# Attention feeding a gated mixture: reordering the first transfers, with batch 1 in half-size units

## The chip, the cores and the metric

The kernel runs on one core of one Trainium2 chip. The metric is the device time of one execution in microseconds (us). The profile is of one execution, with its engines: TensorE (PE, its weight loads PEld), VectorE (DVE), ScalarE (ACT), GpSimd (POOL) and SyncE (SP), which here only issues DMAs.

## The reference

Attention over 8 batches of 8 heads with 576 positions of 64 numbers, in a window of 128 with a linear bias, then a mixture of 8 experts over all 4608 tokens, whose gate is normalised over rows and columns in turn:

```
scores = scale * q @ k.T                      # per batch and head
scores = where(0 <= rel < 128, scores - slope[h] * |rel|, -1e9)
x = softmax(scores) @ v                       # (4608, 512) after joining the heads
P = exp(x @ w_gate - max)
8 times: P /= P.sum(1) + 1e-9;  P /= P.sum(0) + 1e-9;  P *= N / E
out = sum over e of P[:, e] * (relu(x @ w1[e]) @ w2[e])
```

## The kernel before, in words

Every engine's order is the order of the program: it is written out by hand, and the framework adds only waits and buffers. An engine that waits for one operand therefore holds up all that stands behind it.

**Attention.** A batch is 5 blocks of keys (four of 128 positions and a tail of 64), each in two halves of heads, so 10 steps. A step is named (b, at), with at = 0 to 9. Step n of the loop does, in order: the scores of the next steps (`scores`, L385, PE), their exponentials (`exps`, L403, ACT), about 1 us of expert work, the mask (`masks`, L416, DVE), the value products (`values`, L441, PE), the turn of the finished block into `xT` (`turn_x`, L472), and more expert work. Scores run one step or two ahead of the values. In `values`, the batch 0 steps and the first six of batch 1 begin with three spins: products of a constant tile (L225) whose result is written over, there to keep TensorE active. `spin_alone` adds more between the steps.

**q, k and v.** `load_qk` (L245, SP) brings q and k of a batch as two transfers of 1 MB. `cast_qk` (b, j) turns heads 2j and 2j+1 to 16 bits, k on ACT (L260) and q on DVE (L258); `turn_pe` turns them on PE (L324) with the copies on ACT (L339, k) and DVE (L337, q). v comes block by block (`load_v`, L347, SP; `cast_v`, L357 and L358, POOL), the tail of q and k by `load_tail` (L236, SP). In the main loop stand, of this kind: `load_v` six blocks ahead at odd steps, `load_qk(b + 2)` and its tail at (b, 3) and later from b = 1 on, the casts of batch 2 in batch 1, and **the first cast of batch 3 at the end of (1, 8)** (L722). Buffers of v and of the tails are five in number; a load waits until the one it takes is free.

**Experts 0 and 1** run beside the attention. Their weights W1 and W2 are loaded and cast by DMAs that POOL issues (L87, L89), each in POOL's order. A unit is one expert on a range of blocks (a block is 128 tokens): 8 layer-1 atoms of 128 hidden columns (L103: four products each, then a ReLU on ACT, L110), then one layer-2 atom per block (L116: eight products, then a copy on DVE). `Filler` hands atoms out: `take()` gives one layer-2 atom after two of layer 1, `fill(us)` goes on until that time is spent, `hold` keeps layer 2 back, `ready` says how many blocks of `xT` exist, `allowed` which experts. In batches 0 to 2 a step's share is the backlog divided by the steps left to at = 8. PSUM has four buffers for all of these products and the turns.

The units come in this order, where `spans` are ranges (first block, blocks):

```
spans = [(0, 2), (2, 2)] + [(4 * g, 4) for g in range(1, NG)]
order = [(0, 0), (0, 1)]
for n in range(2, len(spans)):
    order += [(0, n), (1, n - 2)]
```

**Ahead of batch 1's scores** the program runs the rest of expert 0 on batch 0, both layers, between the casts and turns of batch 1. The later part of the kernel (the gate, experts 2 to 7) isn't touched.

Of the kernel before, what the change touches and what calls it, by code (L numbers as in the profile page):

```python
# [14 lines left out]
def kernel(  # L15
# [10 lines left out]
    nc = tc.nc  # L26
# [4 lines left out]
    B, H, S, Dh = q.shape  # L31
# [10 lines left out]
    NKB = 5  # L42
# [162 lines left out]
    if True:  # L205
# [23 lines left out]
        def spin_alone(n):  # L229
            spins[0] += 1  # L230
            spin(aps.tile([P, GT], FP32, name=f"psJ_{spins[0]}", tag="pmm", bufs=4), n)
# [6 lines left out]
                )  # L238
            tails[b] = t32

        def load_qk(b):
            q32 = per.tile([P, H, RI * Dh], FP32, name=f"q32_{b}", tag="a8", bufs=8)
            k32 = per.tile([P, H, RI * Dh], FP32, name=f"k32_{b}", tag="a8", bufs=8)
            for t, src in ((q32, q), (k32, k)):
                nc.sync.dma_start(  # L245
                    out=t, in_=src[b, :, 0:SM, :].rearrange("h (p i) d -> p h (i d)", i=RI)
                )
            raw[b] = (q32, k32)

        def cast_qk(b, j):  # L250

            if j == 0:
                c16s[b] = per.tile([P, 2, RI, H, Dh], FP16, name=f"c16_{b}", tag="a8", bufs=8)
            for n in (1, 0):
                src = raw[b][n][:, 2 * j : 2 * j + 2, :].rearrange("p h (i d) -> p i h d", i=RI)
                to = c16s[b][:, n, :, 2 * j : 2 * j + 2, :]
                if n == 0:
                    nc.vector.tensor_copy(out=to, in_=src)  # L258
                else:
                    nc.scalar.copy(out=to, in_=src)  # L260
            if j == NDT - 1:
                raw.pop(b)

        def homes(b):
            qN = asb.tile([P, NDT, SM], FP16, name=f"qN_{b}", tag="qN", bufs=2)
# [156 lines left out]
        def values(b, kb, u):  # L422

            nk, _ = sizes(kb)
            if u == 0:
                xsbs[b, kb] = asb.tile([P, H, Dh], FP16, name=f"xsb_{b}_{kb}", tag="xsb", bufs=3)
            psN = aps.tile([P, GT], FP32, name=f"psN_{b}_{kb}_{u}", tag="pmm", bufs=4)
            if b == 0 or (b == 1 and 2 * kb + u < 6):
                spin(psN, 3)
            psN = psN[:, 0 : 4 * Dh + 4].rearrange("p (h d) -> p h d", h=4)  # L430
            ops = []
            for y in range(2):
                for hb in range(2):
                    hh = 2 * y + hb
                    if kb > 0:
                        ops.append((hh, pts[b, kb - 1, u][:, 2 * hb + y, P : P + nk], vs[b, kb - 1][:, 4 * u + hh, 0 : Dh + 1]))
                    ops.append((hh, pts[b, kb, u][0:nk, 2 * hb + y, 0:nk], vs[b, kb][0:nk, 4 * u + hh, 0 : Dh + 1]))
            if kb == NKB - 1:
                ops = ops[0::2] + ops[1::2]
            for i, (hh, lhsT, rhs) in enumerate(ops):  # L440
                nc.tensor.matmul(  # L441
                    out=psN[0:nk, hh, :],
                    lhsT=lhsT,
                    rhs=rhs,
                    start=(i == 0),
                    stop=(i == len(ops) - 1),
                )
            if kb > 0:
                pts.pop((b, kb - 1, u))
            rden = asb.tile([P, 4], FP32, name=f"rden_{b}_{kb}_{u}", tag="rden", bufs=2)  # L450
            nc.vector.reciprocal(out=rden[0:nk, :], in_=psN[0:nk, :, Dh])
            nc.vector.tensor_tensor(
                out=xsbs[b, kb][0:nk, 4 * u : 4 * u + 4, :],
                in0=psN[0:nk, :, 0:Dh],
                in1=rden[0:nk, :].unsqueeze(2).to_broadcast([nk, 4, Dh]),
                op=ALU.mult,
            )
# [59 lines left out]
            nc.vector.tensor_copy(out=yo, in_=ps)  # L517
            stores.append((e, blk, yo))

        spans = [(0, 2), (2, 2)] + [(4 * g, 4) for g in range(1, NG)]  # L520
        order = [(0, 0), (0, 1)]
        for n in range(2, len(spans)):
            order += [(0, n), (1, n - 2)]
# [91 lines left out]
        load_first()  # L615
        spin_alone(20)
        make_mask(range(4))
        cast_v(0)
        load_weights(0, 0, 1)
        cast_v(1)  # L620
        load_weights(0, 1, 2)
        cast_v(2)
        nc.gpsimd.dma_start(out=wg_sb, in_=moe_w_gate.rearrange("(dt p) e -> p dt e", p=P))
        cast_v(3)
        cast_v(4)
        load_qk(1)
        load_tail(1)
        load_v(NKB)


        steps = [(b, kb, u) for b in range(B) for kb in range(NKB) for u in range(2)]
# [18 lines left out]
        for n, (b, kb, u) in enumerate(steps):  # L650
            nxt = steps[n + 1] if n + 1 < len(steps) else None
            at = 2 * kb + u
            left = ((8 if b < XPE else 10) - at) % 10 + 1
            budget = filler.backlog() / (11 if (b, at) == (XPE, 0) else left)
            if b == 0:
                budget = 1.0 if at in (6, 7) else 0.0
            if nxt:
                if nxt[0] < XPE and nxt[1:] == (RI - 2, 1):
                    turn_pe(nxt[0], 0, NDT)
                if nxt == (1, 0, 0):  # L660
                    filler.ready = RI
                    while filler.l1 or filler.todo[0][1] < RI:
                        filler.take()
                    filler.hold = False
                    spin_alone(8)
                    filler.fill(3.6)
                    cast_qk(1, 0)
                    cast_qk(1, 1)
                    for j in range(NDT):
                        turn_pe(1, 1, j)  # L670
                        turn_pe(1, 0, j)
                        if j < 2:
                            cast_qk(1, j + 2)
                        filler.fill(1.0)
                if n == 0:
                    scores(*nxt)
                elif nxt[2] == 0:
                    scores(*nxt)
                    scores(*nxt[:2], 1)
                exps(*nxt)  # L680
            got = filler.fill(1.0) if b else 0.0
            if nxt:
                masks(*nxt)
            values(b, kb, u)
            if n > 0 and u == 0 and by_pe(steps[n - 1][0]):
                turn_x(*steps[n - 1][:2])
            if u == 1 and n // 2 + NKB < B * NKB:
                cast_v(n // 2 + NKB)
            filler.fill(budget - got)
            if at == 0 and b > XPE:  # L690
                filler.ready = 4 * b
            if at < 8 and b < XPE:
                filler.ready = 4 * b + at // 2
            if at == 8 and b < XPE:
                filler.ready = 4 * b + 4
            if u == 1 and not by_pe(b):
                turn_x(b, kb)
            if u == 1:
                if kb == 1 and b > 0:
                    gates(4 * b - 4, 4 * b)  # L700
                if n // 2 + NKB + 1 < B * NKB:
                    load_v(n // 2 + NKB + 1)
            if b == 0 and at == 1:
                load_weights(1)
            if b == 1 and at == 4:
                filler.allowed.add(1)
                nc.sync.dma_start(out=ysp[0, 0:RI].rearrange("m p d -> p m d"), in_=first_y[0])
            if (b, at) == (0, 3):
                load_qk(2)
            if (b, at) == (0, 7):  # L710
                homes(1)
            if (b, at) == (1, 3):
                homes(2)
            if b == 1 and 4 <= at <= 7:
                cast_qk(2, at - 4)
            if b == 1 and 5 <= at <= 8:
                turn_pe(2, 1, at - 5)
                turn_pe(2, 0, at - 5)
            if 1 <= b < B - 2 and at == 3:
                load_qk(b + 2)  # L720
            if 1 <= b < B - 2 and at >= 8:
                cast_qk(b + 2, at - 8)  # L722
            if 2 <= b < B - 1:
                if at < 2:
                    cast_qk(b + 1, at + 2)
                if at == 1:
                    turn_qk(b + 1)
                    order_qk(b + 1, 1, range(NDT))
                if at == 5:
                    turn_tail(b + 1)  # L730
                if at in (6, 7):
                    order_qk(b + 1, 0, range(2 * at - 12, 2 * at - 10))
            if b < B - 1 and at == (1 if b > 1 else 5) and b:
                load_tail(b + 1)
            if 10 * b + at >= 66:
                i = 10 * b + at - 66
                if i % 8 == 0:
                    home_last(2 + i // 8)
                (load_w2 if i % 8 < 4 else load_w1)(2 + i // 8, i % 4, 4)
            if (b, at) == (7, 0):  # L740
                todo += sums_of(2, *extras(2))
            if b == 7 and at >= 5:
                some(1)
# [334 lines left out]
```

## Time and profile before

| what | value |
|---|---|
| median of 3 runs | 1058.27 us (1057.51 to 1058.65) |
| the profiled execution's own time | 1056.82 us |
| its span | 1055.0 us |
| PE busy | 1037.6 us, 98% |
| ACT busy | 437.3 us, 41% |
| DVE busy | 631.4 us, 60% |
| POOL busy | 77.4 us, 7% |
| moved by DMA | 98.57 MB |
| k and q of batch 1 landed | 35.5 and 31.5 us |
| W1 and W2 of expert 0 landed | 22.4 and 30.3 us |
| W1 and W2 of expert 1 landed | 52.0 and 59.4 us |

A span is the time between the first and the last recorded instruction; the execution's own time has 1.8 us around it. "Idle before, releaser" in a row is the time that an engine stood before those instructions, and what ended it. "Issue to landing" of a DMA is the time from the start of the instruction that issues it until its last data are there. Starts are in us from the span's start. A matmul row's duration includes the pipeline, so a group of eight is shorter than eight times one; the chain's rows show what a group really takes.

### The profile page before, as it was taken

Reading aid. Unit: us, or ns where it says so; the run is one execution under the profiler, and the core shown is the slowest. Engines: PE = TensorE matmul, PEld = TensorE weight load, DVE = VectorE, ACT = ScalarE, POOL = GpSimd, SP = SyncE. Lnnn points to the kernel's source line nnn. Section 1 sums busy time; section 2 is a strip of 40 time slices with the busy share of each in tenths; the row PEclk is TensorE's granted clock in tenths of the full one; section 3 lists DMA queues with packets and bytes.
Section 4 is the critical chain, followed back from the end, with each engine's and each line's share of the span. In section 5 each row is a group of like instructions: output and inputs, shape, how many; then the busy total and the mean of one; then the engine's idle time right before and its main releaser. Section 6 shows DMA issues by size and latency. Waiting matters only on the chain.

```text
span 1055.0 us, 21321 instructions
## 1 busy us (share of the span) xinstructions
PE 1037.6 (98%) x9094; PEld 808.2 (77%) x9094; DVE 631.4 (60%) x1166; ACT 437.3 (41%) x734; POOL 77.4 (7%) x139
## 2 busy tenths in 40 slices
PE   8999999999999999999999999999999999999998
PEld 5664444454444888888888888888888888888887
DVE  5555666565687665655655655655655555556555
ACT  7655564655332333333333333333333333333332
POOL 2122033234100000000000000000000000000000
PEclk9999999999999999999999999999999999999999
DMA  9997488979991510210210220210220220220240
GB/s 227 248 226 170 105 216 201 202 152 188 180 204 56 106 47 25 71 52 21 71 61 11 71 64 8 71 53 19 71 69 3 71 70 2 71 71 1 71 90 21
DMA packets 166111, 98.57 MB, mean 93 GB/s; under 512 B 84960, under 2 KB 157440, under 8 KB 166016
## 3 DMA queue, kind: packets, MB, share of 16 engines
q1 hardware_dynamic: 151280, 79.21, 28.9%
q0 software_dynamic: 14304, 17.84, 10.2%
q8 instruction: 71, 1.16, 0.4%
q14 instruction: 24, 0.20, 0.1%
q10 hardware_dynamic: 432, 0.16, 0.1%
HBM read 87.74 MB, written 19.02 MB: 101 GB/s over the span
## 4 chain that ended last, share of the span: by engine, by line
PE 90%; DMA 6%; SPq 2%; DVE 1%; ACT 1%; issue 0%; POOL 0%; POOLq 0%; DVEq 0%; ACTq 0%
PE psh L865 35%; PE psS_m L920 31%; PE psy L116 10%; PE psh L103 10%; DMA v<-in_v_dram 4%; PE psN L441 1%; DMA xT<-xsb 1%; PE psS L385 1%; DMA pbc<-ptd 1%; SPq L347 1%; SPq L236 1%; ACT pt L403 0%; DVE yo L517 0%; PE psy L985 0%; DMA k<-in_k_dram 0%
## 5 line engine op out<-in xcount | busy, mean ns | idle before, releaser
L872 ACT ACTIVATE hs<-psh 128x512 f16<-128x512 f32 x432 | 257.9, 597 | 454.5 <-PE psh L865 372.9
L865 PE MATMUL psh<-aux,w1l 128*128 128x256 f16 x2880 | 372.6, 273 | 1.5 <-DVE aux L849 1.5
L865 PEld LDWEIGHTS <-w1l 128*128 128x128 f16 x2880 | 281.7, 98 | 34.5 <-issue 1.7
L920 PEld LDWEIGHTS <-hs 128*128 128x128 f16 x2568 | 251.3, 98 | 29.1
L877 DVE TENSOR_TENSOR hs<-hs 128x1024 f16<-128x1024 f16 x107 | 74.1, 693 | 274.4 <-ACT hs L872 274.4
L920 PE MATMUL psS_m<-w2l,hs 128*128 128x256 f16 x1440 | 186.6, 273 | 0.0
L103 PE MATMUL psh<-xT,w1t 128*128 128x512 f16 (+1 forms) x640 | 139.9, 358 | 2.2 <-ACT hT L110 1.4
L849 DVE TENSOR_TENSOR aux<-xT,pbc 128x1024 f16<-128x1024 f16 x108 | 131.4, 1218 | 3.8 <-DMA pbc<-ptd 3.8
L116 PE MATMUL psy<-w2t,hT 128*128 128x512 f16 x576 | 133.6, 379 | 0.0
L110 ACT ACTIVATE hT<-psh 128x512 f16<-128x512 f32 (+1 forms) x160 | 87.7, 556 | 97.9 <-PE psh L103 96.6
L116 PEld LDWEIGHTS <-hT 128*128 128x128 f16 x576 | 53.9, 98 | 61.0 <-issue 1.0
L103 PEld LDWEIGHTS <-w1t 128*128 128x128 f16 x640 | 57.7, 98 | 50.6 <-issue 5.8
L966 DVE TENSOR_TENSOR acc<-acc,psS_m 128x256 f32<-128x256 f32 (+1 forms) x162 | 74.4, 506 | 12.4 <-PE psS_m L920 11.1
L403 ACT ACTIVATE pt<-psS 128x1024 f16<-128x1024 f32 (+2 forms) x80 | 67.6, 851 | 33.0 <-PE psS L385 28.6
L517 DVE CAST yo<-psy 128x512 f16<-128x512 f32 x68 | 46.9, 690 | 53.7 <-PE psy L116 50.7
L416 DVE TENSOR_TENSOR pt<-pt,mask 128x1024 f16<-128x1024 f16 (+2 forms) x80 | 51.9, 649 | 39.3 <-ACT pt L403 39.0
L865 PE MATMUL psh<-aux,w1t 128*128 128x256 f16 x576 | 74.6, 273 | 0.0
L920 PE MATMUL psS_m<-more,hs 128*128 128x256 f16 x576 | 74.6, 273 | 0.0
L880 DVE TENSOR_TENSOR hs<-hs 128x1024 f16<-128x1024 f16 x107 | 73.2, 684 | 0.0
L865 PEld LDWEIGHTS <-w1t 128*128 128x128 f16 x576 | 56.4, 98 | 6.5
L553 POOL DMA_DIRECT2D w2t<-in_moe_w_dram x2 | 1.8, 878 | 706.5 <-PE psS_m L920 671.0
L441 PEld LDWEIGHTS <-pt 128*128 128x128 f16 (+2 forms) x576 | 28.5, 100 | 25.2 <-issue 6.9
(87 smaller groups left out, 672.3 us busy)
## 6 DMA issues: line engine op xcount, KB each, us to landing
pbc<-ptd SPq DMA_DIRECT2D x108, 128.0 KB, 4.4
y<-ysp SPq DMA_DIRECT2D x36, 256.0 KB, 4.6
ysp<-yo SPq DMA_DIRECT2D x68, 128.0 KB, 3.5
v<-in_v_dram SPq DMA_DIRECT2D x32, 256.0 KB, 3.8
out_dram<-acc SPq DMA_DIRECT2D x31, 256.0 KB, 2.5
q<-in_q_dram SPq DMA_DIRECT2D x7, 1024.0 KB, 7.4
k<-in_k_dram SPq DMA_DIRECT2D x7, 1024.0 KB, 10.4
w2t<-in_moe_w_dram POOLq DMA_DIRECT2D x4, 1024.0 KB, 14.0
```

Source lines behind the costliest of these rows:

```text
L103: nc.tensor.matmul(out=ps[:, 0:nt], lhsT=w1ts[e][:, dt, P * ft : P * ft + P], rhs=xT[:, b0 : b0 + nb, dt, :], start=(dt == 0), stop=(dt == ...
L110: nc.scalar.activation(out=st["hT"][:, ft, 0:nt], in_=ps[:, 0:nt], func=AF.Relu)
L116: nc.tensor.matmul(out=ps, lhsT=st["hT"][:, ft, P * ms : P * ms + P], rhs=w2ts[e][:, ft, :], start=(ft == 0), stop=(ft == NFT - 1),)
L403: nc.scalar.activation(out=pt[0:nk, :, 0 : nk + nn], in_=ps[0:nk, :, :, 0 : nk + nn].rearrange("p a y n -> p (a y) n"), func=AF.Exp, scale ...
L416: nc.vector.tensor_tensor(out=pt[0:nk, :, 0:w], in0=pt[0:nk, :, 0:w], in1=mask[0:nk, hs, 0:w], op=ALU.mult)
L849: nc.vector.tensor_tensor(out=xs(n).rearrange("p (d b t) -> p d b t", d=NDT, b=2), in0=xT[:, 2 * g : 2 * g + 2].rearrange("p b d t -> p d ...
L865: nc.tensor.matmul(out=ps[:, f, :], lhsT=W1L[e][:, dt, P * ft : P * ft + P], rhs=xs(n)[:, HB * dt : HB * dt + HB], start=(dt == 0), stop=( ...
L872: nc.scalar.activation(out=h[n][:, 2 * i : 2 * i + 2, :], in_=ps, func=AF.Relu)
L877: nc.vector.tensor_tensor(out=t[:, NFT : NFT + NF2, :], in0=a[:, 0:NF2, :], in1=a[:, NF2:NFT, :], op=ALU.add)
L880: nc.vector.tensor_tensor(out=t[:, NFT + NF2 : 2 * NFT, :].rearrange("p f n -> p (f n)").rearrange("p (f t) -> p f t", t=P), in0=a[:, :, P ...
L920: nc.tensor.matmul(out=Ms[g, bank][:, half, :], lhsT=left(n, m, f), rhs=W2L[e][RIGHT[m]][:, f, :], start=(e == 2 and f == 0 and half == 0) ...
L966: nc.vector.tensor_tensor(out=a, in0=a, in1=p2, op=op)
```

## The change

It reorders the first transfers and what is computed beside them:

- POOL's queue: W1 of expert 0 after the third v cast instead of after the first; then the gate's weights, two v casts, the casts of q of batch 1 for j = 2 and 3 (moved there from DVE), and only then W2. Expert 1's weights are issued at (0, 7) instead of (0, 1).
- SP's queue: q and k of batch 1 in two halves each, then the first v of batch 1, then its tail. q and k of batch 2 at (0, 9) instead of (0, 3).
- Ahead of batch 1's scores only 8 layer-1 atoms, then one after each of the four turns. Layer 2 is held until (1, 2), expert 1 until (1, 8). No expert work in batch 0's own steps.
- Batch 1 as units of 2 blocks (256 tokens), for both experts.
- Casts of batch 2 at (1, 5) to (1, 7), its turns at (1, 6) to (1, 8), both two at first; fewer spins.

```diff
-        def load_qk(b):
+        def load_qk(b, parts=1):
...
+            w = H // parts
+            for n in range(parts):
+                for t, src in ((q32, q), (k32, k)):
+                    nc.sync.dma_start(
+                        out=t[:, n * w : n * w + w],
+                        in_=src[b, n * w : n * w + w, 0:SM, :].rearrange("h (p i) d -> p h (i d)", i=RI),
+                    )
...
-        def cast_qk(b, j):
+        def cast_qk(b, j, which=(1, 0), pool=False):
...
+                if pool:
+                    nc.gpsimd.tensor_copy(out=to, in_=src)
+                elif n == 0:
...
-            if b == 0 or (b == 1 and 2 * kb + u < 6):
+            if b == 0 or (b == 1 and 2 * kb + u < 4):
                 spin(psN, 3)
...
-        spans = [(0, 2), (2, 2)] + [(4 * g, 4) for g in range(1, NG)]
+        spans = [(2 * g, 2) for g in range(4)] + [(4 * g, 4) for g in range(2, NG)]
...
+        load_qk(1, 2)
+        load_v(NKB)
+        load_tail(1)
         cast_v(0)
+        cast_v(1)
+        cast_v(2)
         load_weights(0, 0, 1)
-        cast_v(1)
-        load_weights(0, 1, 2)
-        cast_v(2)
         nc.gpsimd.dma_start(out=wg_sb, in_=moe_w_gate.rearrange("(dt p) e -> p dt e", p=P))
         cast_v(3)
         cast_v(4)
-        load_qk(1)
-        load_tail(1)
-        load_v(NKB)
+        for j in (2, 3):
+            cast_qk(1, j, (0,), True)
+        load_weights(0, 1, 2)
...
-                budget = 1.0 if at in (6, 7) else 0.0
+                budget = 0.0
...
                     filler.ready = RI
-                    while filler.l1 or filler.todo[0][1] < RI:
+                    spin_alone(6)
+                    for _ in range(NFT):
                         filler.take()
-                    filler.hold = False
-                    spin_alone(8)
-                    filler.fill(3.6)
                     cast_qk(1, 0)
                     cast_qk(1, 1)
                     for j in range(NDT):
                         turn_pe(1, 1, j)
                         turn_pe(1, 0, j)
                         if j < 2:
-                            cast_qk(1, j + 2)
-                        filler.fill(1.0)
+                            cast_qk(1, j + 2, (1,))
+                        filler.take()
...
-            if b == 0 and at == 1:
+            if b == 0 and at == 7:
                 load_weights(1)
-            if b == 1 and at == 4:
+            if (b, at) == (1, 8):
                 filler.allowed.add(1)
+            if (b, at) == (1, 2):
+                filler.hold = False
+            if b == 1 and at == 8:
                 nc.sync.dma_start(out=ysp[0, 0:RI].rearrange("m p d -> p m d"), in_=first_y[0])
-            if (b, at) == (0, 3):
+            if (b, at) == (0, 9):
                 load_qk(2)
...
-            if b == 1 and 4 <= at <= 7:
-                cast_qk(2, at - 4)
             if b == 1 and 5 <= at <= 8:
-                turn_pe(2, 1, at - 5)
-                turn_pe(2, 0, at - 5)
+                for j in ((), (0, 1), (2,), (3,))[at - 5]:
+                    turn_pe(2, 1, j)
+                    turn_pe(2, 0, j)
+                for j in ((0, 1), (2,), (3,), ())[at - 5]:
+                    cast_qk(2, j)
```

More of the change, by code (lines that the diff above doesn't have):

```diff
@@ L239, in load_tail @@
             tails[b] = t32
-        def load_qk(b):
+        def load_qk(b, parts=1):
             q32 = per.tile([P, H, RI * Dh], FP32, name=f"q32_{b}", tag="a8", bufs=8)
             k32 = per.tile([P, H, RI * Dh], FP32, name=f"k32_{b}", tag="a8", bufs=8)
[L244 to L247, printed above, removed]
+            w = H // parts
[5 more added lines that the diff above has]
+                    )
             raw[b] = (q32, k32)
-        def cast_qk(b, j):
-            if j == 0:
+        def cast_qk(b, j, which=(1, 0), pool=False):
+            if b not in c16s:
                 c16s[b] = per.tile([P, 2, RI, H, Dh], FP16, name=f"c16_{b}", tag="a8", bufs=8)
-            for n in (1, 0):
+            for n in which:
                 src = raw[b][n][:, 2 * j : 2 * j + 2, :].rearrange("p h (i d) -> p i h d", i=RI)
                 to = c16s[b][:, n, :, 2 * j : 2 * j + 2, :]
-                if n == 0:
+                if pool:
+                    nc.gpsimd.tensor_copy(out=to, in_=src)
+                elif n == 0:
                     nc.vector.tensor_copy(out=to, in_=src)
@@ L260, in cast_qk @@
                     nc.scalar.copy(out=to, in_=src)
-            if j == NDT - 1:
-                raw.pop(b)
         def homes(b):
```

## The prediction

> **What bounds the kernel now.** I began with the slices of the page: TensorE is busy nearly everywhere, but the DMA row is full over the first three slices and only then falls.
>
> ```profile
> PE   8999999999999999999999999999999999999998
> ...
> DMA  9997488979991510210210220210220220220240
> ```
>
> One slice is 26.4 us, so the transfers fill the engines up to about 75 us, and that is the stretch the change works on. TensorE's "busy" is no measure there: it holds spins and modelled latencies. I therefore counted products and gave each its row from the chain of waits: a layer-1 atom of 256 tokens (four products) 0.435 us, since eight take 0.87; a layer-2 atom 1.73. With the smaller products at their back-to-back spacing, TensorE has done about 23.2 us of useful work at 44 us and about 44.9 at 73.6: some 20.8 us are lost before 44, and 7.9 more before 73.6. Beyond 85 us the loss is small per stretch. The second number is what the change can win; the first belongs to batch 0's dependent chain. The busy time by stretch shows the transfers beside it (share of the 16 DMA engines and GB/s at the end):
>
> ```profile
> 26.50:44.00 17.50, 16.36 (x134) 10.89 (x132) 7.54 (x15) 10.28 (x22) 3.58 (x8) 1.00 1.11 257
> 44.00:60.00 16.00, 13.50 (x182) 10.57 (x181) 10.30 (x28) 11.83 (x22) 0.19 (x1) 1.00 1.17 219
> 60.00:75.00 15.00, 13.97 (x130) 8.84 (x130) 9.26 (x21) 7.11 (x17) 3.11 (x10) 1.00 0.89 250
> 75.00:100.00 25.00, 24.58 (x202) 12.45 (x201) 13.44 (x32) 15.32 (x25) 8.17 (x15) 1.00 0.58 139
> ```
>
> Next, which transfers are just in time: the waits of ScalarE from 25 to 80 us (total, times, longest), then two of SyncE's issues in the timeline (start, us):
>
> ```profile
> ACT c L260 <- DMA k<-in_k_dram: 4.2, 2, 3.2
> ```
>
> ```profile
> 14.52 2.02 SPq L245 DMA_DIRECT2D k<-in_k_dram  x1
> 16.64 11.25 SPq L236 DMA_DIRECT2D t<-in_q_dram  x1
> ```
>
> The k casts waited 3.2 us for batch 1 (k landed at 35.5) and 1.0 us for batch 2 (landed at 53.3). SyncE itself stood 11.25 us in one issue behind such a k: its queue is never empty. The third k, batch 3's, is issued at 61.53 and takes 10.6 us (first line below, tile k between 60 and 75 us), so it lands at 72.1. Its first cast is in the chain (second fence: start, us, what):
>
> ```profile
> DMA to landing us min/median/max: 10.6/10.6/10.6
> ```
>
> ```profile
> 72.98 0.70 DVE yo L517
> 73.69 0.00 issue
> 73.69 0.63 ACT c L260
> 74.32 0.01 issue
> 74.33 0.29 PE psS L385 x2
> 74.61 0.97 PE psh L103 x4
> ```
>
> It starts 1.6 us after its data: no wait now, but that little slack is what decides my forecast.
>
> **The change, part by part.** I write (b, at) for a step and follow the program order.
>
> Batch 0. W1 goes behind the third v cast, so its issue moves from 12.1 to about 16 us. The v transfers lose that competitor: v of blocks 3 and 4 landed at 21.5 and 25.1 under W1, and should now land near 17. That removes the 1.3 us wait of the value product on L358 near 21 us. The two fills of 1.0 us at steps 6 and 7 go too, four atoms or 1.74 us of useful work put off. Batch 0 ends near 23.9 instead of 26.5: 2.6 earlier, 1.74 of it deferred, so 0.9 is won.
>
> W1 late. W1 landed 10.3 us after its issue (tile w1t); it now runs beside q and k instead of v, and I keep the 10.3: about 26.5. Six spins (0.65) and then a wait of about 2 us. Bounds: no wait if it lands at 24.5, 4 us if it takes the 13.7 of expert 1's W1; I take 2, from the 10.3 row. Two spins fewer (2 x 0.109) vanish in it.
>
> Casts and turns of batch 1. k's first cast follows eight ReLUs on ScalarE, so it starts near 30 although the data is there at 26. ScalarE then has 4 casts, 4 evacuations and 4 ReLUs at about 0.52, 0.48 and 0.40: 5.6 us, TensorE 3.5 beside it. Scores of batch 1 come near 35.5 instead of 43.9, with 4 layer-1 and 4 layer-2 atoms undone (8.7 us): 0.3 us worse or better, nothing. The two q casts on GpSimd take VectorE's 2 x 0.42 away. No row has this form on GpSimd: between 0.61 (its v cast) and 1.18 each (its strided kN copy). I take 0.61, for the same types; either is hidden, since W2 behind them lands by 41 and is first used at (1, 3), near 41 to 42.
>
> Steps of batch 1. The deferred atoms fill them: 0.87, 0.87, 0, 1.74, 1.74, 2.61, 2.61, 3.48, 1.74 us for steps 0 to 8, from the filler's rule. That is 15.7 us of work where waits and spins stood, and two steps lose their three spins (0.65). Of the 7.9 us lost from 44 to 73.6, about 6 would go. Units of 256 tokens cost TensorE nothing (eight products 0.87, four of 512 0.86); ScalarE pays 2 x 385 - 599 = 171 ns for each of 16 pairs, 2.7 us, hidden where it is not the bound.
>
> What is late next. Without a wait, TensorE would reach the end of (1, 8) at 60 to 61 us instead of 73.4, having done 20.9 us of expert atoms (12 of layer 1, 5.2 us, before the scores, and 15.7) where today's program has done 27.8 (32 x 0.435 + 8 x 1.73): 6.96 us are pushed behind that point. But there stand the casts of batch 3's q and k. Everything that goes ahead of that k today still goes ahead of it: four batches of q and k, 13 blocks of v, two tails, both experts' weights. Expert 1 behind v of batch 1 does not help, because its packets (from 43.8 us in today's packet records, 5.5 after the issue) start near 44 again, the v in front of it landing near 39, and they interleave with q and k. What can be saved is the part of the DMA engines that idles: shares of 0.97 from 35 to 40 and 0.84 from 60 to 65 against about 1.15 elsewhere, so 5 x 0.16 + 5 x 0.27 = 2 us at the most. I take 1.6: **batch 3's k lands near 70.5**. Before it, the k of batch 2, now behind v of block 10 and beside expert 1's W1, lands at 54 to 58, wanted at 47.5; TensorE can run 4 us more on what is queued and then stands. This first stall costs nothing by itself, for the second wait absorbs it as long as that k is there by 60.
>
> Behind the blocked cast on ScalarE wait the exponentials of (2, 0) and every ReLU; TensorE stops when its four PSUM buffers are full, after scores, three layer-1 atoms and the value products, about 2.2 us beyond the point. After the landing: cast 0.6, exponential 1.0, first ReLU 0.4, so TensorE goes on at 72.5. Today it does so at 74.6, with the scores (0.45) behind it. **Sum:** 72.5 - 74.6 + 6.96 - (2.2 - 0.45) = +3.1 us. ScalarE then has the backlog of short ReLUs, 0 to 0.8 us: 0.4. Together **+3.5 us** on the profiled execution: 1056.8 (span 1055.0) becomes 1060.3. That run lies 1.45 under the median shown, so on the median 1058.3 + 3.5 = **1061.8**. Each us on that landing is a us on the end; it breaks even at about 67.
>
> **The rivals.** (1) *The transfers do not bind* (faster): the k of batch 3 lands by 62 to 63, or TensorE gets there later than I think with its waits filled. For it: 7.9 us stand open, and v interleaved with weights moved at only 219 GB/s. Against it: the shares above. Then -0.9 and -6 with about 1 us lost elsewhere: 1052.3. It decides where that k lands under 66.5. Chance 0.22. (2) *It evens out*: that k lands at 66 to 68.5, from faster halves or shorter idling: 1058.3, chance 0.21. (3) *A cold restart*: TensorE's first 20 products took 4.24 us for 2.18 at the later pace, so a start from rest costs 2.1 us; if it comes back after a stall of 4 to 5 us it adds that to my forecast: 1063.9. The longest wait after the start today is 1.3 us, with 109 ns spacing behind it, so the rows can't say whether 4 us suffice. Chance 0.12. The Trainium skill, "TensorE: Matmul & The Clock Gate", "HAM oscillation — how this bites in real kernels", asks for no idle gap above about 3.4 us; by that rule this rival holds, and the trace agrees only in the half-speed first spins. (4) *It does not do what it says*: the q casts wait for q's second half and W2 comes later than 42, so layer 2 of batch 0 stalls at (1, 3). That is absorbed by the same later wait; the time is the forecast's.
>
> **How the numbers follow.** Forecast 0.45 (its own range 1059.5 to 1065, from landings of 68.5 to 72 and 0 to 0.8 behind), (3) 0.12, (2) 0.21, (1) 0.22. Slower by over 0.2% (above 1060.4; about what a measurement of this kernel can tell from no change) 0.56, within 0.22, faster 0.22. The range 1053 to 1066 leaves out the full gain's lower half and two cold restarts.
>
> **What would show it.** Right: in the changed profile the casts L260 wait for k twice in batch 1, the last ending near 70; TensorE has gaps of several us before 58 and before 72; v of blocks 3 and 4 is no longer waited for; the slices beyond the sixth are as now. Wrong: no wait of L260 on k at (1, 8), or k of batch 3 landing under 66.

## The result and the profile after

The changed kernel takes **1062.62 us** (median of 5 executions, 1061.54 to 1065.42) against 1058.27 for the kernel before (5 executions, 1057.21 to 1060.23): a ratio of 1.0043, 95% interval 1.0024 to 1.0062. It is 4.35 us slower; 3.5 was forecast. The profiled execution took 1061.54 us, with a span of 1059.8, 4.8 longer than before's.

The slices of the changed kernel, TensorE, granted clock and DMA, 26.5 us each:

```profile
PE   7889999999999999999999999999999999999998
...
PEclk9999999999999999999999999999999999999999
DMA  9996399779992501201201211211220220220240
```

The DMA row is full in the first three slices, as before, and TensorE's first three slices fell by one digit each. The clock row seems clean: a slice of 26.5 us and a digit of a tenth hide what a finer view shows below. The stretches that were shown of before, in the same view of the changed kernel (length; busy time of PE, PEld, DVE, ACT, POOL with instructions; granted clock; DMA share; GB/s):

```profile
26.50:44.00 17.50, 13.80 (x134) 10.66 (x135) 5.23 (x10) 12.06 (x27) 6.08 (x14) 0.90 1.09 213
44.00:60.00 16.00, 13.89 (x158) 9.14 (x157) 10.64 (x27) 8.08 (x15) 0.21 (x2) 1.00 1.14 240
60.00:75.00 15.00, 14.14 (x147) 10.22 (x145) 9.72 (x21) 9.41 (x22) 3.37 (x9) 1.00 1.04 274
75.00:100.00 25.00, 22.63 (x218) 15.17 (x216) 11.46 (x26) 14.62 (x31) 6.14 (x8) 1.00 0.60 153
```

Two stretches are worse: 26.5 to 44, with a granted clock of 0.90, and 75 to 100, with 2.0 us less of busy TensorE. Between them the transfers are as dense as before. To count what these busy times hide, I took from each stretch its length less its products at their back-to-back spacing in the trace of before (spins count as nothing). This "lost time" in us:

| stretch | before | after |
|---|---|---|
| 0 to 25 | 17.1 | 17.9 |
| 25 to 50 | 7.2 | 10.3 |
| 50 to 75 | 5.0 | 4.4 |
| 75 to 100 | 1.7 | 3.7 |
| 100 to 200 | 6.7 | 7.0 |

After has lost 5.6 us more by 200 us, and 4.8 more by the end. The gap opens at two places, 25 to 50 and 75 to 100.

**The first place: W1.** TensorE in the timeline of the changed kernel (start, us, instruction, in brackets the idle time before it and what ended it):

```profile
24.23 0.82 PE L225 MATMUL psJ<-ones 128*128 128x256 f16 x6
29.12 5.13 PE L103 MATMUL psh<-xT,w1t 128*128 128x256 f16 x32 [4.08 <-DMA w1t<-in_moe_w_dram]
```

After six spins TensorE stands 4.08 us for W1, and then its 32 products take 5.13 us. The granted clock says why. The same time cut into pieces of 3.41 us, columns as above:

```profile
25.34:28.75 3.41, 0.00 (x0) 0.00 (x0) 0.11 (x1) 0.00 (x0) 1.97 (x3) 1.00 1.24 216
28.75:32.16 3.41, 3.04 (x15) 2.17 (x16) 0.00 (x0) 1.02 (x3) 0.67 (x2) 0.50 1.31 224
32.16:35.57 3.41, 2.43 (x25) 1.97 (x24) 0.00 (x0) 2.93 (x8) 0.00 (x0) 1.00 1.21 197
```

One piece has no product, and the next runs at half speed. So the mean clock of the run, 0.998, is one such piece, not noise.

**The later waits for k**, where the forecast put the stall, are small. ScalarE's waits from 25 to 80 us (total, times, longest), then its two casts that waited:

```profile
ACT c L265 <- DMA k<-in_k_dram: 1.8, 2, 1.4
```

```profile
56.41 1.14 ACT L265 CAST c<-k 128x512 f16<-128x512 f32 x2 [1.42 <-DMA k<-in_k_dram]
```

```profile
69.95 0.62 ACT L265 CAST c<-k 128x512 f16<-128x512 f32 x1 [0.42 <-DMA k<-in_k_dram]
```

The k of batch 2 landed at 56.31 and that of batch 3 at 69.88, each 0.1 before its cast: both still decide, but TensorE now comes late enough to meet them.

**The second place** shows in TensorE's waits from 24 to 100 us (total, times, longest). The second line is new: a layer-2 product waits for the last ReLU of its own unit. I took the reason to be that a half-size unit leaves nothing between the two; experiments 4 and 10 bear that out only in small part.

```profile
PE psh L103 <- DMA w1t<-in_moe_w_dram: 4.1, 1, 4.1
PE psy L116 <- ACT hT L110: 3.0, 4, 1.0
```

### The profile page after: what moved, and what is told of

Same layout as the page of the kernel before. It is cut to its first block, busy times and chain, and to the rows that moved or that the text cites. A ratio compares the mean times of both kernels' runs of the same rounds, so it can differ in the third digit from the quotient of the medians.

```text
span 1059.8 us, 21455 instructions
## 1 busy us (share of the span) xinstructions
PE 1038.7 (98%) x9150; PEld 813.5 (77%) x9150; DVE 629.8 (59%) x1164; ACT 439.1 (41%) x750; POOL 80.8 (8%) x141
## 2 busy tenths in 40 slices
DMA packets 166143, 98.57 MB, mean 93 GB/s; under 512 B 84992, under 2 KB 157472, under 8 KB 166048
## 4 chain that ended last, share of the span: by engine, by line
PE 84%; DMA 1%; DVE 0%; issue 0%; SPq 0%; DVEq 0%
PE psh L872 35%; PE psS_m L927 31%; PE psy L116 8%; PE psh L103 8%; PE psN L444 1%; DMA pbc<-ptd 1%; PE psS L388 1%; PE psy L992 0%; PE psG L494 0%; DVE yo L520 0%; DVE aux L856 0%; PE psX L475 0%; PE psC L797 0%; DVE pt L419 0%; PE psP L812 0%
## 5 line engine op out<-in xcount | busy, mean ns | idle before, releaser
L116 PE MATMUL psy<-w2t,hT 128*128 128x512 f16 x576 | 134.1, 380 | 3.1 <-ACT hT L110 3.0
L110 ACT ACTIVATE hT<-psh 128x512 f16<-128x512 f32 (+1 forms) x176 | 89.9, 521 | 110.1 <-PE psh L103 108.3
L103 PEld LDWEIGHTS <-w1t 128*128 128x128 f16 x704 | 64.7, 99 | 51.9 <-issue 4.7
L116 PEld LDWEIGHTS <-hT 128*128 128x128 f16 x576 | 53.9, 98 | 64.2 <-issue 5.1
L520 DVE CAST yo<-psy 128x512 f16<-128x512 f32 x68 | 46.8, 690 | 60.2 <-PE psy L116 60.2
L406 ACT ACTIVATE pt<-psS 128x1024 f16<-128x1024 f32 (+2 forms) x80 | 67.7, 851 | 28.7 <-PE psS L388 26.5
L872 PEld LDWEIGHTS <-w1t 128*128 128x128 f16 x576 | 56.3, 98 | 6.6
L927 PEld LDWEIGHTS <-aux 128*128 128x128 f16 x428 | 41.8, 98 | 4.9
```

Source lines behind the costliest of these rows:

```text
L103: nc.tensor.matmul(out=ps[:, 0:nt], lhsT=w1ts[e][:, dt, P * ft : P * ft + P], rhs=xT[:, b0 : b0 + nb, dt, :], start=(dt == 0), stop=(dt == ...
L110: nc.scalar.activation(out=st["hT"][:, ft, 0:nt], in_=ps[:, 0:nt], func=AF.Relu)
L116: nc.tensor.matmul(out=ps, lhsT=st["hT"][:, ft, P * ms : P * ms + P], rhs=w2ts[e][:, ft, :], start=(ft == 0), stop=(ft == NFT - 1),)
L406: nc.scalar.activation(out=pt[0:nk, :, 0 : nk + nn], in_=ps[0:nk, :, :, 0 : nk + nn].rearrange("p a y n -> p (a y) n"), func=AF.Exp, scale ...
L872: nc.tensor.matmul(out=ps[:, f, :], lhsT=W1L[e][:, dt, P * ft : P * ft + P], rhs=xs(n)[:, HB * dt : HB * dt + HB], start=(dt == 0), stop=( ...
L927: nc.tensor.matmul(out=Ms[g, bank][:, half, :], lhsT=left(n, m, f), rhs=W2L[e][RIGHT[m]][:, f, :], start=(e == 2 and f == 0 and half == 0) ...
```

## The experiments

Theory A is the forecast's: the transfers ahead of the k of batch 3 bind, and a stall that is taken away at one place comes back at the next late transfer. Rival B: the wait for W1 is a plain loss of its own. To these came theory C, on the units of 256 tokens. All ratios are against the kernel before on the same chip; where kernels of different chips are set side by side, the difference is that of their ratios, times 1058.

**1. W1 early again.** The changed kernel, with W1 issued where it was before.

```diff
         cast_v(0)
+        load_weights(0, 0, 1)
         cast_v(1)
         cast_v(2)
-        load_weights(0, 0, 1)
```

> The changed kernel with one thing undone: W1 of expert 0 is issued after the first v cast again, as before. Theory A (q and k of batches 2 and 3 bind): TensorE's 4.1 us wait for W1 goes, but k of batch 3 still lands near 70 us, so the wait moves to the casts of k (L265) at (1, 5) and (1, 8), several us each; at most 1 us is won against the changed kernel: 1061.5 to 1062.5. Rival B (the wait for W1 and the slow products behind it set the time): 4 us or more are won, 1057 to 1058.5, and the casts of k wait no longer than now (1.4 and 0.4 us).

Measured: 1063.30 us, ratio 1.0056 [1.0041, 1.0070]. The wait for W1 is gone, its 32 products take 3.66 us, and nothing is won; the time is even 0.8 above the range that theory A gave. ScalarE's wait for k from 25 to 80 us, TensorE's longest from 24 to 100, and the clock in the pieces around them:

```profile
ACT c L265 <- DMA k<-in_k_dram: 7.9, 1, 7.9
```

```profile
PE psy L116 <- ACT hT L110: 8.9, 3, 7.2
```

```profile
54.35:57.76 3.41, 0.00 (x0) 0.00 (x0) 0.00 (x0) 0.00 (x0) 0.00 (x0) 1.00 1.16 214
57.76:61.17 3.41, 0.36 (x1) 0.10 (x1) 0.65 (x2) 2.39 (x5) 0.00 (x0) 0.50 1.22 197
61.17:64.59 3.42, 3.42 (x12) 1.43 (x11) 0.93 (x4) 0.00 (x0) 0.31 (x1) 0.50 1.18 287
```

Five engines are empty for a whole piece while DMA moves 214 GB/s: the core waits for the k of batch 2, which lands at 58.55. The row names a ReLU as what ended TensorE's wait, but that ReLU stood behind the blocked cast on ScalarE. Two pieces at half speed follow, which theory A had not priced. The stall moved as A says and B falls, in this kernel; but only the first of the two waits that A named came. The k of batch 3 landed at 71.51, and its cast, held up by then, didn't wait for it.

**2. The same, with batch 3's casts one step later.** Two of batch 3's casts each at (2, 0) and (2, 1), where the change has one at (1, 8) and (1, 9) each and the rest at (2, 0) and (2, 1).

```diff
-            if 1 <= b < B - 2 and at >= 8:
+            if 2 <= b < B - 2 and at >= 8:
                 cast_qk(b + 2, at - 8)
+            if b == 2 and at < 2:
+                cast_qk(3, 2 * at)
...
-                    cast_qk(b + 1, at + 2)
+                    cast_qk(b + 1, at + 2 if b > 2 else 2 * at + 1)
```

> As the kernel with the early W1, and besides the four casts of q and k of batch 3 stand two each at (2, 0) and (2, 1) instead of one each from (1, 8) on, about 5 us later in the program. Theory A: the second stall goes too, 2 to 3 us are won against the early W1 alone: 1058.5 to 1060, the cast of k of batch 2 still waiting. Rival B: no difference between the two (within 0.5 us on the span).

Measured: 1062.68 us, ratio 1.0042 [1.0026, 1.0058], beside 1.0056 for the first experiment: no difference that can be told. The expectation missed, and for a reason: the k that was waited for (3.3 us in this profile) is that of batch 2, which this edit doesn't touch. Alone it says nothing about batch 3.

**3. TensorE kept active across the wait for W1.** The changed kernel, with 44 spins instead of 6.

```diff
-                    spin_alone(6)
+                    spin_alone(44)
```

> The changed kernel with 44 spins instead of 6 in front of expert 0's first products, so that TensorE is not at rest while it waits for W1. If the 32 products behind that wait (5.13 us now) are slow because TensorE rested 4 us, they take 3.5 us now. Theory A: the 1.6 us won there are lost again at the casts of k, the time stays within 0.7 us of the changed kernel's. Rival B: 1.6 us are won on the end, 1061.0. If rest is not the cause, the 32 products still take about 5.1.

Measured: 1061.87 us, ratio 1.0043 [1.0028, 1.0057]. The 32 products took 3.67 us instead of 5.13, so the rest ahead of them was what slowed them. But the wait for the k of batch 2 rose from 1.4 to 4.6 us, and a half-speed piece came behind that one, at 60.2. What was saved at W1 went into that wait, as theory A says; the end is the same within the noise.

**4. Expert 1's batch 1 as one unit of 512 tokens**, everything else as changed.

```diff
+        ranges = [(e, (4, 4) if (e, n) == (1, 2) else spans[n]) for e, n in order if (e, n) != (1, 3)]
         filler = Filler(
-            (e, *spans[n], lambda e=e, n=n: ...)
-            for e, n in order
+            (e, *s, lambda e=e, s=s: ...)
+            for e, s in ranges
         )
```

(The dots stand for the rest of the two lines.)

> The changed kernel with batch 1 of expert 1 as one unit of 512 tokens again; expert 0 stays in halves. Theory: between 75 and 100 us the changed kernel loses 2 us more than the kernel before, since a half unit's first layer-2 atom follows right behind its last ReLU (L116 waits 3.0 us for L110 in all). Eight ReLUs less and one such place less should give back 0.5 to 1.5 us: 1061.3 to 1062. Rival: those waits come from the batch 0 units, which are halves in both kernels, run later; then nothing changes.

Measured: 1060.93 us, ratio 1.0027 [1.0013, 1.0040]: 1.7 us under the changed kernel's, a little more than expected, but the two intervals overlap, so the gain is not clear of the noise. In its profile the lost time from 75 to 100 us is 3.1 instead of 3.7, and 1.3 less is lost by 200. Of the changed kernel's four waits of L116 for L110, at 58.58, 76.97, 86.16 and 96.20 us, only the last (0.54 us) is gone. The first three stay, so they are not this unit's.

**5. Without expert 1's loads.** The first experiment, with expert 1 computing from expert 0's weights.

```diff
-                load_weights(1)
+                w1ts[1], w2ts[1] = w1ts[0], w2ts[0]
```

> The early W1, and expert 1's weights are not loaded: expert 1 computes with expert 0's weights, so its part of the output is left out. 2 of the transfers, some 12 us of the DMA engines, are gone. Theory A (transfers bind batches 2 and 3): k of batch 2 lands by 51 and that of batch 3 by 60, no cast waits for k, TensorE reaches the end of (1, 8) near 62, and the time falls by 6 to 9 us against the early W1 alone, to 1054 to 1057. Rival B (program order, not data): the time stays within 2 us of the early W1's 1063.

Measured: 1055.46 us, ratio 0.9971 [0.9960, 0.9983], 9.0 under the first experiment by the ratios (0.0085). The k of batch 2 lands at 50.06 and that of batch 3 at 58.57, and one wait of 1.1 us is left. Same products, 2 MB fewer to move (96.47 instead of 98.57): this is the plainest proof that the transfers bind. No execution lost clock here, while every one of the first experiment's did, so the 9.0 us hold the stall and its half-speed pieces together.

**6. Expert 1's loads later.** The first experiment, with those loads at (1, 1) instead of (0, 7).

```diff
-            if b == 0 and at == 7:
+            if (b, at) == (1, 1):
                 load_weights(1)
```

> The early W1, and expert 1's loads issued at (1, 1) instead of (0, 7), so that q and k of batch 2 go ahead of most of them. Nothing else. Theory A: k of batch 2 lands at 50 to 52 instead of 58.5, its cast waits under 2 us instead of 7.9; k of batch 3 lands at 70 to 72 as ever and its cast at (1, 8) waits 4 to 7 us in its place; the time gains 0 to 2 us against the early W1 alone. Rival: the first wait alone counted, and 5 us or more are won.

Measured: 1062.10 us, ratio 1.0035 [1.0023, 1.0047]. The profiled execution, at 1065.96, is the slowest of its 11. In it the k of batch 2 lands at 53.28 and costs 0.55 us; the k of batch 3 lands at 72.77 and costs 6.3 (the third wait, 1.0, is for the k of batch 1):

```profile
ACT c L265 <- DMA k<-in_k_dram: 7.9, 3, 6.3
```

Nearly as long as the first experiment's 7.9, at the next batch. This is the stall that the prediction described, at the place it named, in a kernel where nothing earlier had already taken its time.

**7. All of it together.** The sixth, with batch 3's casts two each at (2, 1) and (2, 2), their turns following them, and expert 1's batch 1 as one unit (the edit of the fourth).

```diff
...
+            if b == 2 and at in (1, 2):
+                cast_qk(3, 2 * at - 2)
+                cast_qk(3, 2 * at - 1)
...
```

> The early W1, expert 1's loads at (1, 1), the casts of batch 3's q and k two each at (2, 1) and (2, 2) with their turn at (2, 2), and batch 1 of expert 1 as one unit of 512. Theory A: with each consumer behind its data nothing waits for long; TensorE has lost 25 to 28 us at 75 instead of 32.6, and the time is 1053 to 1056, under the kernel before. Rival B: the order costs by itself and it stays above 1060.

Measured: **1055.49 us** (12 executions), ratio 0.9973 [0.9958, 0.9989]; it beats both kernels. ScalarE's only wait for k left:

```profile
ACT c L265 <- DMA k<-in_k_dram: 0.6, 1, 0.6
```

The k of batch 3 lands at 68.84 and is first wanted at 76.99. Lost time by 100 us is 28.8, against 31.0 before and 36.3 after.

**8. The kernel before, without expert 1's loads**, by the edit of the fifth.

> The kernel before without the loads of expert 1's weights (it computes expert 1 with expert 0's weights, that part of the output is left out). Theory A: the kernel before is at the same bound but waits little for it (1.0 us for k of batch 2, 1.3 us for a v): 1 to 3 us are won, 1055.5 to 1057.5. Rival: if it wins 5 us or more, the kernel before loses much more to its transfers than its waits show.

Measured: 1055.38 us, ratio 0.9967 [0.9955, 0.9979]: 3.5 us, a little over what was expected, where the changed order with W1 early gained 9.0 from the same edit. Part of the 3.5 is clock: none of these executions lost any, and 13 of the 29 of the kernel before did. Among executions at a full clock it is 1055.4 against 1057.4, or 2.0 us. That the kernel before loses so much less to these transfers fits its small waits for k; its consumers stand about where the data come.

**9. The seventh, with W1 late** (behind the third v cast, as in the change).

> The best kernel so far (early W1, expert 1's loads at (1, 1), batch 3's casts at (2, 1) and (2, 2), expert 1 of batch 1 as one unit) with W1 put back behind the third v cast, as the change has it. Alone, the early W1 won nothing in the changed kernel (1063.3 against 1062.6). Theory A: it won nothing because k of batches 2 and 3 caught TensorE afterwards; here they do not bind (their casts wait 0.6 us in all), so the late W1 costs its whole stall: 4 us of waiting and 1.5 of slow products less 1.3 for the v wait that it saves, 3 to 4.5 us: 1058.5 to 1060. Rival: the early W1 is worth nothing in itself and the time stays at 1055 to 1056.

Measured: 1059.98 us, ratio 1.0014 [1.0002, 1.0027], 4.3 us over the seventh by the ratios. From 24 to 100 us:

```profile
PE psh L103 <- DMA w1t<-in_moe_w_dram: 3.6, 1, 3.6
```

The 32 products take 5.33 us, with a half-speed piece from 29.45. So here W1's place is worth 4.3 us, where the first experiment showed it to be worth nothing. Both are true: a stall costs in full once nothing behind it takes the time back.

**10. The kernel before, with batch 1 in units of 256 tokens**, and nothing else of the change.

```diff
-        spans = [(0, 2), (2, 2)] + [(4 * g, 4) for g in range(1, NG)]
+        spans = [(2 * g, 2) for g in range(4)] + [(4 * g, 4) for g in range(2, NG)]
```

> The kernel before with batch 1 in units of 256 tokens for both experts, nothing else of the change. Theory: what the 256 token units cost between 75 and 100 us is theirs, not that of the deferred work: 0.5 to 2 us slower than the kernel before, 1058.5 to 1060, with more wait of layer 2 (L116) for the ReLU (L110). Rival: the early start of expert 0's first half in batch 1 pays for it, and the time is the same or lower by up to 1 us.

Measured: 1063.01 us, ratio 1.0049 [1.0032, 1.0067]: 5.2 us, where at most 2 were expected. This one edit costs as much as the whole change. No wait of TensorE between 48 and 125 us is longer than 1.4 us, yet its clock is halved three times in the profile, which is of the slowest of the six executions (mean clock 0.994, the others 0.996 to 0.998). The first time, from 13.15 us, lies in batch 0, ahead of the units. The pieces around the later two:

```profile
50.70:54.11 3.41, 1.79 (x33) 1.37 (x32) 2.43 (x9) 1.61 (x3) 0.00 (x0) 1.00 1.19 210
54.11:57.52 3.41, 3.41 (x23) 2.56 (x22) 1.30 (x4) 1.89 (x4) 0.00 (x0) 0.50 1.20 197
112.14:115.55 3.41, 1.91 (x22) 0.94 (x21) 3.38 (x10) 0.38 (x1) 0.00 (x0) 1.00 1.29 304
115.55:118.96 3.41, 2.63 (x15) 1.13 (x14) 1.78 (x5) 2.14 (x3) 0.67 (x2) 0.50 1.01 179
118.96:122.38 3.42, 3.42 (x10) 1.19 (x10) 1.03 (x3) 0.60 (x1) 1.31 (x4) 0.50 0.25 70
```

Pieces in which TensorE is busy for 1.8 to 1.9 of 3.41 us are followed by half speed, the second by two pieces. This gave theory C: the units cost little by themselves, and the half-speed pieces the rest. The wait that was expected isn't there: from 44 to 200 us no layer-2 product (L116) waits for a ReLU.

**11. The tenth, with spins there:** ten each at (1, 5), (2, 9) and (3, 0).

```diff
+            if (b, at) in ((1, 5), (2, 9), (3, 0)):
+                spin_alone(10)
             got = filler.fill(1.0) if b else 0.0
```

> The kernel before with batch 1 in units of 256 tokens (5.3 us slower than before, with the granted clock at half from 54.1 to 57.5 and from 115.6 to 122.4 us), and ten more spins each at (1, 5), (2, 9) and (3, 0), in front of the expert work, where TensorE stood in the 3.4 us ahead of those two stretches. Theory C (most of the 5.3 us is the clock at half speed, which follows a stretch in which TensorE works only about half the time): the half stretches go, and 3 to 5 us come back although 3.3 us of spins are added: 1058.5 to 1060.5. Rival: the loss is the ReLUs' and the copies'; the stretches may go but the time stays at 1062 to 1064 or grows by the spins.

Measured: 1061.58 us (12 executions), ratio 1.0034 [1.0019, 1.0048], 1.6 under the tenth, over what theory C gave, and not clear of the noise of the two. The profiled execution has no half-speed piece at all and a span 5.9 us shorter, but it is not typical. The mean granted clock of each execution sorts them: in 4 of the 12 it is 1.000, with a median of 1059.9, and the other 8 have 1062.3; in the tenth it is never 1.000. The kernel before, on the same chip, has a median of 1057.2 in its 16 executions at 1.000. So with a full clock the units and the 30 added spins together still cost **2.7 us**. How much of it the spins are (3.3 us of products, if none of them falls into a wait) was not measured. That the units cost something of their own shows in the profile from 75 to 100 us, where none of the added spins stands: a count of lost time as above gives 1.9 us more than before's, here and in the tenth. Theory C was right that half-speed pieces are part of the loss; its share stays open.

**12. The seventh, with expert 1's batch 1 in halves again.**

> The best kernel with expert 1's batch 1 in halves again, as the change has it. In the changed kernel that was worth 1.7 us (1062.6 against 1060.9). Theory: the same here, 0.5 to 2 us slower than the best: 1056 to 1057.5, by L116 waiting for L110. Rival: a stretch at half clock comes with it, as in the kernel before with halves, and it is 3 us or more: 1058.5 and above.

Measured: 1057.17 us (12 executions, 1054.04 to 1064.57), ratio 0.9989 [0.9973, 1.0005]: 1.7 over the seventh, inside the expected range, though the two intervals overlap. At a full clock the medians are 1056.9 (9 executions, 1054.0 to 1058.9) and 1054.1 (7 of the seventh's, 1052.2 to 1056.0), 2.8 apart (the kernel before at a full clock: 1057.2 and 1057.4 beside them). Its waits of L116 for L110 have one of 0.54 us at 100.0 that the seventh's lack, as in experiment 4. Its profiled execution, at 1064.57, is its slowest, and tells something else:

```profile
ACT c L265 <- DMA k<-in_k_dram: 8.2, 1, 8.2
```

The order of the loads is the seventh's. But here SyncE issued the k of batch 2 at 41.33 us and it landed at 58.19, beside expert 1's W1; in the seventh's profile it was issued at 39.89 and landed at 49.52, ahead of it. In both the POOL issue of that W1 started within 0.2 us of 44.1. An issue 1.4 us later came in 8.7 us later. The other runs with that W1 behind the k fit: 3.2 us ahead of W1's issue the k took 8.8 us (experiment 6), 2.6 us ahead of it 14.4 (experiment 9).

## Why the forecast was right, and where its steps were wrong

**The kernel is slower in part for the reason given:** in the stretch where transfers bind, an order that brings TensorE early to its data makes it stand. Experiments 1, 5 and 6 show it. The other part is the units of 256 tokens, which the forecast had at next to nothing and which alone cost the kernel before 5.2 us (experiment 10). The landing that the sum rested on, k of batch 3 at 70.5, was measured at 69.88. But the sum came out near the truth partly by luck, through errors that cancel. Step by step:

- *Batch 0.* v of blocks 3 and 4 landed at 16.9 and 18.2 (about 17 forecast), the wait for v is gone, and batch 0 ended at 24.2 (23.9). Right.
- *"W1 late"* is **the step that failed**: "about 26.5 ... a wait of about 2 us", from the 10.3-us row. W1 landed at 29.08, 12.8 us after its issue, its first packet starting 4.2 us behind it (2.1 before). The wait was 4.1, beyond my upper bound of 4. That bound was also added up wrongly: 16 + 13.7 = 29.7, less 23.9 and 0.65 of spins, is a wait of 5.1, and the row of 13.7 would have covered what came. And the restart at half speed, rival (3), came here, where I hadn't priced it: 5.13 - 3.67 = 1.5 us more. The term was 5.6, not 2.
- *Casts, turns, W2.* Two q casts on GpSimd took 1.41 us, 0.7 each (0.61 taken, bounds 0.61 to 1.18); W2 landed at 38.3 and was first used at 46.2, hidden as said, so rival (4) fell. Scores of batch 1 came at 39.5, not 35.5; 3.6 of these 4 us are the error of W1's term.
- *"What is late next."* The k of batch 2 landed at 56.3 (54 to 58 forecast), but the waits there were 1.4 and 0.4 us where the forecast had two of several us. TensorE, held up at W1, came late to both. I had written that the first stall is absorbed by the next; the same holds one step earlier, and I had not followed it there. Experiment 1 shows the chain without W1's stall: 7.9 us at the first k. So of the signs that I named, the two waits of the casts came, the last ending near 70, and TensorE's gaps of several us before 58 and 72 did not: after W1's, the longest was 1.35 us. (Two small slips of the working: the first packet of expert 1's W1 before, read at 43.8 us, starts at 43.3, and 27.8 less 20.9 is 6.9, not 6.96.)
- *"Units of 256 tokens cost TensorE nothing ... hidden where it is not the bound."* Wrong: 5.2 us in the kernel before (experiment 10). From 75 to 100 us the changed kernel lost 3.7 us, before's profile 1.7; I had 0.4 for that backlog. I compared products with products, and left out what stands between them. Layer 2 close behind a unit's last ReLU is a small part of it, one wait of 0.54 us in experiments 4 and 12; half-speed pieces are another; the rest is open.
- *Rivals (1) and (2)* fell on the landings: 69.88 is beyond the 66 to 68.5 that either needed.

On rival (3): in the changed kernel a wait of 4.08 us left a piece of 3.41 us empty, and the next 3.41 us ran at a clock of 0.50. The Trainium skill, "TensorE: Matmul & The Clock Gate", "HAM oscillation — how this bites in real kernels", asks for no idle gap above about 3.4 us; the trace agrees. But experiment 10 goes further than that sentence: a clock halved behind pieces more than half busy, with no wait over 1.4 us.

The kept traces say which pieces these are. The busy share doesn't: one of 0.53 in experiment 10 (at 50.7 us) was followed by half speed, one of 0.52 in experiment 6 (at 41.2) and one of 0.50 in experiment 10 (at 153.1) by full speed. Busy time includes the modelled ends of products. So I counted the time in which TensorE streams: each product at its back-to-back spacing at a full clock (0.109 us for 256 columns, 0.215 for 512, 0.055 for 128, 0.029 for 65), and once where two 64-row products start 3 ns apart and run side by side. Over the pieces of all 14 profiles from 4 us on, some 4,280, this sorts them without an exception. (A piece at half speed counts by the same spacing, so that equal shares are equal work.) The 16 that streamed at most 0.35 of their length were followed by half speed, and all others, from 0.39 up, by full speed. The pieces of experiment 10 at 50.7 and 112.1 us streamed 0.35 and 0.26 of theirs. It also says why some stalls bring two half-speed pieces: the piece in which the work came back streamed too little once more (0.05 to 0.32, four cases).

The terms, undone one after the other from the changed kernel on (medians in us; the steps by the ratios; each row holds the edits above it):

| kernel | median | step | ratio to before |
|---|---|---|---|
| after | 1062.62 | | 1.0043 |
| W1 early (1) | 1063.30 | +1.4 | 1.0056 |
| expert 1's loads later (6) | 1062.10 | -2.2 | 1.0035 |
| batch 3's casts later (12) | 1057.17 | -4.9 | 0.9989 |
| expert 1's batch 1 in one unit (7) | 1055.49 | -1.7 | 0.9973 |

A step carries the noise of two ratios, 2.0 to 2.5 us, so -4.9 stands clear of it, -2.2 barely, and +1.4 and -1.7 do not. The first two steps together are about nothing (-0.8): they move the stall along the chain of late transfers, and only the third lets it out at the end. By experiment 9, W1's step is worth 4.3 us when it is taken last.

**What stays open.** What the 256-token units cost at a full clock, and by what: the spins of experiment 11 stand in its 2.7 us, and the 2.8 of experiment 12 rests on 9 and 7 executions. Expert 0's half units alone were not measured, nor the cast of q on GpSimd by itself.

## What to carry to other kernels

Where transfers bind, taking away one stall only moves it to the next just-in-time load: list every landing of the stretch beside the time at which its consumer is ready, and move all consumers behind their data before judging any single edit. An edit undone alone can look worthless there, since the next late transfer takes its gain; undo it again once the others are settled. A stall that leaves TensorE empty for several us costs more than its length, so look at the granted clock in pieces of a few us, not at the run's mean or the slices. A piece need not be empty for that: count what TensorE streams in it, not its busy time.

## What the runs showed of the hardware

- The granted clock changes in pieces of 3.41 us, and a stall of several us is followed by one or two of them at 0.50. One makes 32 products take 5.13 instead of 3.67 us. A mean clock of 0.998 is the whole sign of it in a run's numbers, and yet the kernel before, on the chip of experiments 11 and 12, takes 1059.7 at 0.998 (6 executions) against 1057.2 at 1.000 (16).
- What sorts the pieces is how much of each TensorE streams. In these 14 profiles at most 0.35 was always followed by half speed, and 0.39 or more always by full speed; a busy share of 0.53 stands on the one side and one of 0.50 on the other. No piece streamed between 0.35 and 0.39, so where the border lies between them isn't known.
- A load issued by POOL can start late: W1's first packet came 4.2 us after its issue in the changed kernel, where three halves of q and k had been issued ahead of it and had not landed, and 2.1 before. Why wasn't tested.
- The k of batch 2, issued 1.4 us later in one profile than in another, landed 8.7 us later, beside another queue's 1-MB load instead of ahead of it (experiments 7 and 12).
